# The written order of the attention steps, in a fused attention and mixture-of-experts kernel

## The chip, the cores and the metric

One NeuronCore of a Trainium2 chip runs the whole program. The metric is the device time of one execution in microseconds (us); less is better.

## The reference, cut to what matters

```python
q_s = exp(q - max(q, axis=-1)); q_s /= sum(q_s, axis=-1)        # softmax over the head dimension
k_s = exp(k - max(k, axis=2));  k_s /= sum(k_s, axis=2)         # softmax over the sequence
kv  = einsum('bhsd,bhse->bhde', k_s, v)
x   = einsum('bhsd,bhde->bhse', q_s, kv)                        # 8 batches, 8 heads, 576 tokens, 64 wide
x   = x.transpose(0, 2, 1, 3).reshape(4608, 512)
expert = argmax(x @ w_gate); gate = softmax(x @ w_gate)[expert] # 8 experts, top one
y[token] = gate * (relu(x @ w1[expert]) @ w2[expert])           # 512 -> 1024 -> 512
```

All inputs and the output are float32.

## The kernel before, in words

The program has two stages. The first is the attention with the routing, batch after batch (0 to 7). The second runs the experts over the routed rows, expert after expert, and is a stretch of matmuls that TensorE works through without a pause.

In the first stage nothing is scheduled at run time. The work is cut into 780 named steps, each on one engine, and the string `ORDER` lists the names in the order in which the instructions are written. Each name stands for the next step of its kind, by batch and then by part. An engine runs its own instructions strictly in the written order, and each waits for its inputs and for its buffers, so what stands behind a waiting instruction on that engine waits too. Between engines the order has no force of its own.

Below, KV.4.3 is part 3 of batch 4 of step KV. The steps, with their lines:

- SyncE issues the loads: LK (keys, L170; three buffers, so K of batch b waits for the KV steps of batch b-3), LV (values, L174; one buffer, so V of a batch waits for VP and VQ of the batch before), LQ (queries, L186; two buffers), CD (gate weights), CZ (zero rows), WG (eighths of the first expert's w1, L677), IL (the first expert's rows, L721), SW and VG (the first expert's w2, L689).
- Keys: KM0 and KM1 (VectorE, maxima over a partition's tokens, L316, L317, L320), KM2 (TensorE transposes, L325), KM3 (VectorE, L329), KM4 (TensorE spreads the maxima, L334), KS (VectorE subtracts, four parts, L350), KE (ScalarE exp, L354), KV (TensorE, L370, L375), N0 and N1 (VectorE, the denominator, L382, L385), N2 (ScalarE writes the scaled kv, L392), G0 to G3 (the product of kv with the gate weights: TensorE L399, ScalarE L403, TensorE L409, ScalarE L413).
- Values: VP, VQ (ScalarE copies, L178, L181).
- Queries: QM (VectorE, row maxima, L443), QS and QSR (GpSimd subtracts, L449, L455), QE (ScalarE exp of one slice, L460), TR and TL (TensorE transposes, L494), EX and EL (ScalarE, L489, L498).
- Output tiles: MM (TensorE, L509, L512, L515; it needs EX and G3), RE and EV (VectorE evicts, L519, L523, L527). MM has two output buffers: a tile waits for the EV of the tile two before it.
- Routing: LS, R0, R8, R1, R3, R4, R6, RB, RC, RD (VectorE, L577 to L620), R9 (ScalarE, L609), R5 (TensorE, L598 to L601), RH and PU (GpSimd, L624 to L632). PU scatters the rows of one tile to their expert's place in HBM; between two scatters GpSimd writes a dummy (L629).
- First expert: WH (ScalarE, L681) and WL (GpSimd subtracts, L686) split w1 into a high and a low part; IC and ID count its rows; IT, IH, IX bring its rows in; L1, L2, L3 (TensorE L740, ScalarE L745, VectorE L748) are its first layer's first five parts; VH, VL split w2.
- WM are 40 matmuls of constants at the start and WE five at the end (TensorE, L703, L708); nothing reads them.

The scatters of batch 7 come after the stage. At its end stands a barrier of all engines (L966), which also waits until the scatters have landed. Then TensorE goes on with the first expert: L740 again, L1111, and the transposes of L1028, for which the rows of the next step must have been read back from HBM.

Of the kernel before, what the change touches and what calls it, by code (L numbers as in the profile page):

```python
# [1592 lines left out]
```

## Time and profile before

| | us |
|---|---|
| three executions | 574.37, 574.82, 576.01 |
| median | 574.82 |
| the profiled execution, its own time | 575.68 |
| its span, first to last instruction | 573.9 |
| TensorE busy in the span | 544.8 (95%) |
| VectorE busy in the span | 314.1 (55%) |
| ScalarE busy in the span | 256.3 (45%) |
| GpSimd busy in the span | 147.7 (26%) |

The span leaves out 1.8 us of the execution's time, before the first and after the last instruction. Shares of busy time are means over two unlike stages. In the timeline rows, a bracket at the end is the idle time of the engine just before the instruction and what ended it; DVE is VectorE, ACT ScalarE, POOL GpSimd, PE TensorE, PEld its weight load, SPq the issue of a transfer by SyncE.

### The profile page before, as it was taken

To read this page: it belongs to the slowest core of one execution; us is meant where nothing else is said; L and a number is where in the kernel's file an instruction comes from. 1 tells how busy PE (TensorE), PEld (TensorE's weight loads), DVE (VectorE), ACT (ScalarE), POOL (GpSimd) and SP (SyncE) were. 2 spreads that over 40 slices of the span, in tenths; PEclk is the share of its full clock that TensorE was granted. 3 is DMA by queue.
4 is the path that set the end of the run, shared out by engine and by line. 5 is a ranking of instruction groups with operands and counts; after the bars stand their busy time and mean duration, and the time that the engine had idled before them with its cause. 6 is when DMAs were issued, how large, how long until landed. Compare 5 with 4: busy or idle time off the path is not lost.

```text
span 573.9 us, 12179 instructions
## 1 busy us (share of the span) xinstructions
PE 544.8 (95%) x3891; PEld 482.7 (84%) x3892; DVE 314.1 (55%) x644; ACT 256.3 (45%) x602; POOL 147.7 (26%) x237
## 2 busy tenths in 40 slices
PE   6799887998999999999999999999999999999995
PEld 2577776897978989899898989897999899898973
DVE  5899989797781431635223141436734473647250
ACT  0699987786412322534131323334725262534341
POOL 4224697685751010110201001002010201120021
PEclk9799999999999999999999999999999999999998
DMA  8989999753668932041931202031195229324700
GB/s 268 334 270 318 318 344 365 242 216 129 241 243 273 365 76 59 0 110 40 396 95 53 57 18 74 19 74 37 46 374 154 83 72 396 64 64 161 314 36 10
DMA packets 70272, 97.70 MB, mean 170 GB/s; under 512 B 9052, under 2 KB 50526, under 8 KB 69600
## 3 DMA queue, kind: packets, MB, share of 16 engines
q1 hardware_dynamic: 63760, 77.19, 42.2%
q0 software_dynamic: 5904, 19.03, 8.7%
q10 hardware_dynamic: 576, 1.07, 0.5%
q8 instruction: 19, 0.31, 0.2%
q14 instruction: 13, 0.11, 0.1%
HBM read 75.31 MB, written 22.34 MB: 170 GB/s over the span
## 4 chain that ended last, share of the span: by engine, by line
PE 75%; issue 0%; POOL 0%; ACT 0%; DVE 0%; POOLq 0%; SPq 0%
PE py L1059 31%; PE pt L1043 16%; PE ph L1043 16%; PE py L1111 3%; PE ph L740 3%; PE py L1099 1%; PE xp L512 1%; PE pt L1087 1%; PE qT L494 0%; PE pt L740 0%; PE pt L1072 0%; PE ph L1072 0%; PE pt L1028 0%; PE pt L726 0%; PE xp L515 0%
## 5 line engine op out<-in xcount | busy, mean ns | idle before, releaser
L1059 PE MATMUL py<-w2h,hid 128*128 128x512 f32 x528 | 164.9, 389 | 0.0
L1059 PEld LDWEIGHTS py<-w2h,hid 128*128 128x128 f32 x528 | 99.1, 188 | 20.4
L1414 POOL DMA_INDIRECT out<-yt,ix x36 | 40.7, 1131 | 284.6 <-ACT yt L1225 278.0
L1059 PE MATMUL py<-w2l,hid 128*128 128x512 f32 x264 | 102.9, 390 | 0.0
L1321 DVE SCALAR_TENSOR_TENSOR hid<-pt,hid 128x384 fp32r<-128x384 f32 x52 | 28.9, 556 | 125.1 <-ACT hid L1235 124.9
L1225 ACT ACTIVATE yt<-py,ga 128x512 f32<-128x512 f32 (+1 forms) x38 | 25.7, 678 | 134.0 <-PE py L1059 120.0
L1321 DVE SCALAR_TENSOR_TENSOR hid<-ph,hid 128x384 fp32r<-128x384 f32 x52 | 29.0, 558 | 53.3 <-ACT hid L1235 53.2
L1059 PEld LDWEIGHTS py<-w2l,hid 128*128 128x128 f32 x264 | 49.5, 188 | 9.8
L1310 DVE STREAM_TRANSPOSE xx<-xb 128x1536 f32<-128x1536 f32 x13 | 37.9, 2914 | 18.2 <-issue 18.2
L512 PE MATMUL xp<-kx,qTs 128*128 128x146 f32 x256 | 43.7, 312 | 2.1 <-ACT kx L413 2.0
L632 POOL DMA_INDIRECT xs<-xr,posi x36 | 37.0, 1029 | 22.0 <-issue 20.2
L512 PEld LDWEIGHTS xp<-kx,qTs 128*128 128x128 f32 x256 | 35.9, 194 | 5.8 <-ACT kx L413 2.4
L1043 PE MATMUL pt<-xh,w1h 128*128 128x384 f32 (+4 forms) x208 | 39.8, 313 | 0.2 <-issue 0.2
L1043 PE MATMUL ph<-xh,w1h 128*128 128x384 f32 (+4 forms) x208 | 39.6, 312 | 0.0
L1043 PE MATMUL pt<-xl,w1h 128*128 128x384 f32 (+4 forms) x208 | 39.6, 312 | 0.0
L1043 PE MATMUL ph<-xh,w1l 128*128 128x384 f32 (+4 forms) x208 | 39.6, 312 | 0.0
L1043 PE MATMUL pt<-xh,w1l 128*128 128x384 f32 (+4 forms) x208 | 39.6, 312 | 0.0
L1043 PE MATMUL ph<-xl,w1h 128*128 128x384 f32 (+4 forms) x208 | 39.5, 312 | 0.0
L1234 ACT ACTIVATE hf<-pt 128x64 f32<-128x64 f32 x52 | 11.7, 225 | 55.8 <-PE pt L1043 43.3
L1234 ACT ACTIVATE hf<-ph 128x64 f32<-128x64 f32 x52 | 11.7, 224 | 53.0 <-PE ph L1043 53.0
L1043 PEld LDWEIGHTS pt<-xh,w1h 128*128 128x128 f32 x208 | 33.6, 189 | 1.7 <-issue 0.7
L1043 PEld LDWEIGHTS pt<-xl,w1h 128*128 128x128 f32 x208 | 33.3, 189 | 0.0
(269 smaller groups left out, 988.8 us busy)
## 6 DMA issues: line engine op xcount, KB each, us to landing
raw<-in_moe_w SPq DMA_DIRECT2D x10, 2048.0 KB, 13.7
rawc<-in_moe_w SPq DMA_DIRECT2D x5, 2048.0 KB, 8.5
kt<-in_k SPq DMA_DIRECT2D x14, 640.0 KB, 8.3
xb<-xs SPq DMA_DIRECT2D x32, 192.0 KB
qt<-in_q SPq DMA_DIRECT2D x8, 640.0 KB, 8.8
vs<-in_v SPq DMA_DIRECT2D x8, 640.0 KB, 7.7
qt<-in_q SPq DMA_DIRECT2D x8, 512.0 KB, 7.3
vs<-in_v SPq DMA_DIRECT2D x8, 512.0 KB, 8.5
```

The source lines that it names most:

```text
L512: nc.tensor.matmul(xv[:, c, :KW], o.qT[i][:, c, :], kx[:, c, :], **flags)
L632: s = nc.gpsimd.indirect_dma_start(out=xs, out_offset=bass.IndirectOffsetOnAxis(ap=n.pi[:, t - t0:t - t0 + 1], axis=0), in_=xr[:, t, :], i ...
L740: m = nc.tensor.matmul(ph, wt[:, c, f * P:(f + 1) * P], xt[:, c, :], start=(n == 0), stop=(n == 3 * NC - 1))
L1043: m = e.matmul(ph, wt[:, c, f * P:(f + 1) * P], xt[:, c, :w], start=(n == 0), stop=(n == 3 * NC - 1))
L1059: m = e.matmul(g.PY[u], ht[:, f, u * P:(u + 1) * P], wt[:, f, :], start=(n == 0), stop=(n == 3 * NF - 1))
L1087: m = e.matmul(y[d * SLIM:(d + 1) * SLIM, :DM // 2], g.HT[:, i * P + s * SLIM:i * P + (s + 1) * SLIM], g.RAW2[:, 4 * s + i, d * DM // 2:(d ...
L1111: m = e.matmul(g.PY[u], ht[:, f, u * P:(u + 1) * P], wt[:, f, :], start=(n == 0), stop=(n == 3 * NF - 1))
L1225: m = e.activation(g.YT[u][:, :w], g.PY[u][:, :w], AF.Copy, scale=g.GA[:, u + thin:u + thin + 1]).wait_op(sPY[u], cu[u], GE)
L1234: e.activation(g.HF[:, f, :], g.PH[f][:, 2 * P:2 * P + SLIM], AF.Relu).wait_op(sPH[f], it, GE)
L1310: e.transpose(g.XX, g.XB.rearrange("p t (a c) -> p c t a", c=NC)).wait_op(sB, bs, GE)
L1321: e.scalar_tensor_tensor(g.HL[:, f, :], g.PH[f][:, :W], 0.0, g.HH[:, f, :].bitcast(F32), op0=ALU.max, op1=ALU.subtract).wait_op(sHH[f], it ...
L1414: e.indirect_dma_start(out=g.out, out_offset=bass.IndirectOffsetOnAxis(ap=g.IX[:, u:u + 1], axis=0), in_=g.YT[u], in_offset=None, bounds_c ...
```

## The change

Only the string `ORDER` differs. Every step is still there once; no step, tile, buffer or loop changes. What moves, engine by engine, where it is spoken of later:

| engine | before | after |
|---|---|---|
| PE, start | 15 WM, KM2.0, KM4.0, 22 WM, KM2.1, KM4.1, WM, TR.0.0, KV.0.0 to KV.0.3, TL.0 | 30 WM, KM2.0, 3 WM, KM4.0, 2 WM, KM2.1, KM4.1, TL.0, KV.0.0, KV.0.1, TR.0.0, 3 WM, KV.0.2, KV.0.3 |
| ACT, start | VQ.0, VP.0, QE.0.0, KE.0.0, ... , QE.0.2, EL.0, N2.0, EX.0.1, G1.0, G3.0, QE.0.3, VP.1 | KE.0.0 to KE.0.3, VP.0, VQ.0, EL.0, KE.1.0, QE.0.0 to QE.0.3, EX.0.0, ..., N2.0, EX.0.1, G1.0, G3.0, VP.1 |
| ACT, batches 4 to 6 | KE.5.2, VQ.6, G3.4, KE.5.3, VP.6 | KE.5.1, KE.5.2, G3.4, VQ.6, KE.5.3, KE.6.0, VP.6 |
| DVE, batch 5 | QM.5, KM3.6, ..., KS.6.3, ..., N0.5, R3.3, N1.5, R4.3, EV.4.0 | QM.5, EV.3.3, KM3.6, ..., KS.6.3, R8.3, RE.4.0, R1.3, EV.4.0, R3.3, R4.3, RC.3, N0.5 |
| DVE, batch 7 | R6.4, LS.5, R0.5, R8.5, R1.5, R3.5, R4.5, QM.7, N0.7, RE.6.0, N1.7, RB.5, EV.6.0 | LS.5, R0.5, R8.5, R1.5, QM.7, N0.7, N1.7, RE.6.0, EV.6.0, RE.6.1, R6.4, EV.6.1, ID, R3.5, T4, RE.6.2, EV.6.2, R4.5 |
| POOL, batch 2 | QS.1.0, QSR.1, QSR.2, QS.1.1, WL (1st), QS.2.0, QS.2.1 | QS.1.0, QSR.1, QS.1.1, QS.2.0, QSR.2, RH.0, WL (1st), QS.2.1 |
| POOL, batches 4 to 7 | PU.3.0, WL (6th), ..., PU.4.3, WL, WL, QS.7.0, QSR.7 | PU.3.0, ..., PU.4.3, WL, WL, WL, QSR.7, QS.7.0 |
| POOL, end | RH.5, QS.7.1, RH.6, PU.5.0 to PU.5.4, IN, PU.6.0, PU.6.1, RH.7, RH.7, PU.6.2, PU.6.3 | RH.5, QS.7.1, IN, RH.6, PU.5.0 to PU.5.4, RH.7, PU.6.0, RH.7, PU.6.1, PU.6.2, PU.6.3 |
| SyncE, end | LV.6, LK.7 (1st half), WG, LQ.6, LK.7 (2nd half), WG, LV.7, LQ.7, WG, IL | WG, LV.6, WG, WG, LQ.6, LK.7, LV.7, LQ.7, IL |

The diff:

```diff
@@ -33,25 +33,25 @@
 WARM_END = 5
 ON_ACT = (1, 1, 1, 1, 1, 1, 1, 1)
 ORDER = """
-WM WM WM WM WM WM WM WM WM WM WM WM LK WM WM LK LK LK KM0 KM0 LK LK WM LQ LQ LV LV KM1 KM2 KM3 CS KM4 KM0 VQ LK LK LQ KS KM0 KS
-CD WM WM WM WM WM WM WM WM WM WM WM LQ VP WM KM1 WM WM WM WM WM WM WM WM QM QS KS WM LV WM QE KE KE QE KE KS QSR KM2 KM3 KM4 KS
-KS KS WM TR KV KS KE KE EX QE KM0 KM0 KV KV KV N0 TL WM N1 KM1 KM2 KM3 EL TR QM N2 EX G0 KM4 KS QS QS LV KS KS G1 G2 WM G3 MM QE
-RE VP KS EV VQ LK KE LK KM0 KM0 LQ LQ KE KE KE KE TR MM RE KV WG LV EX QE QE QSR KV KV KV N0 N1 TR TR MM EX EV EX TR KM1 QE KM2
-QM N2 MM EX RE KM3 EV RE G0 QE EV LS R0 G1 QSR WH KM4 KS KS KS KS LV QS G2 WL VQ TL G3 MM RE LK VP KE EL KV MM KV KE LK KM0 TR
-WG LQ LV QS KV TR EV KE KE LQ R8 KM0 R1 KM1 LV KE KV N0 R3 EX EX WG KE LK N1 R9 KM2 RE EV KM3 QE N2 QE MM QS RE R4 EV TR QM KM4
-KS EX WH WL QSR KS KS R5 WG MM RE RB VQ KS EV MM RE R6 VP G0 LK G1 CZ KE KE QS WH WH QE KV KV EV LV LV KV TR TR EX TR G2 RC WL
-QE EX LS R0 KV LQ LQ KM0 R8 N0 G3 N1 TR KE N2 R1 RD R3 KM0 WG MM MM R4 RE KM1 R5 EX EV RE RB KM2 KM3 EV R6 MM VQ EX R9 RD RE EV
-LK VP LV G0 G1 QE MM WH RH TR TR WL PU EX QE PU PU PU RE RC QS EX QM KV KV TR EV QE QE KM4 KE KS WL LS QSR KS G2 KE QS R0 LV LK
-G3 KV KV EX N0 KS KS MM MM KE RE R8 TR QE VP EV VQ EX LQ LQ LV LV R1 N1 RE R3 EV RH PU PU PU TL EL QE MM LK WG KM0 TR MM R4 EX
-R5 RE KM0 EV PU R9 TR PU RC N2 EX RB MM G0 G1 RE TR QE EX RH R6 RD KM1 QS KM2 KV KV EV PU G2 QE QM KE VQ KM3 KM4 G3 MM QS PU KE
-VP RE WH EV KS KS KS TR LS LQ LQ KS R0 QSR EX LK WG PU PU KE LV KV KE MM KV RE R8 R1 N0 TR R3 N1 R4 RH R9 KE EX QE EV RC TR EX
-RE N2 LV R5 MM RB EV RD MM G0 QE QE QM KV TR G1 KV KE G2 QS RE EV KV EX PU WH KM0 G3 RE KM0 TR EV R6 KV QE LS N0 R0 N1 R8 KM1 R1
-EX MM MM TR N2 R9 RE R3 WL EX R4 R5 EV RB RE RD VP VQ PU EV KM2 KM3 MM RC RE PU TR EX LQ EV QSR KM4 KS KE MM KS RE PU KE PU G0
-G1 LQ KS KE RH QS EV MM RE KS EV QE R6 KV G2 KV PU QS PU G3 QE QE TR EX LS KV KE TR R0 PU PU WG EX WH R8 WL WL MM TL EL R1 KV R3
-R4 QM N0 RE N1 R5 TR QS QSR RB EV MM QE TR RE EX EV MM N2 G0 RE EV EX RD TR MM RE QE QE EX G1 IC ID TR QE G2 TR G3 EX EV LS R0
-MM R6 R8 R1 R3 R9 RH QS IL EX R4 QE RH IT IT RE RC PU PU PU PU R9 SW VG RC MM EV PU IH IH IX VG R6 RE TR EX IX MM EV R5 TR EX RE
-EV IT LS IH IX MM RE MM RB EV L1 R0 R8 R1 RE VH EV T4 R3 LS R0 R8 R1 R9 IN RD PU L2 IM L3 L1 R4 R3 VG R4 R6 L1 VL R6 VH L2 L2 R9
-L3 VG VH T0 L3 T1 PU L1 VL R5 RB RC RC L2 L3 L1 R5 RB RD RH RH RD L2 L3 PU PU WE WE WE WE WE
+WM WM WM WM WM WM WM WM WM WM WM WM WM WM WM WM WM WM WM WM WM WM WM WM WM WM WM WM WM WM LK LK KM0 LK LK KM0 KM1 LK LK KM2 KM3
+WM WM WM LQ CS KM4 KS KE KM0 KS KM0 KS KE KS KE KE KM1 LQ QM WM WM KM2 KM3 KM4 KS KS QSR KS KS LV LV TL LK VP CD LK LQ LQ VQ LV
+EL KE LV KV QS KM0 KV KM0 TR QS QE QE QE QE WM WM WM KV KV EX KM1 N0 N1 WM KM2 WM LK LK TR KE KE LQ KM3 N2 G0 QM EX G1 TR QS KM4
+KS KS KS QSR G2 G3 MM MM VP KS VQ KV RE QE EX QE EV KM0 RE KE QE QE LQ TR KV KV KM0 EX KE KE LV LV EV KV N0 TR TR WG EX KM1 N1
+N2 MM EX QM KM2 KM3 LK LK MM G0 G1 RE VQ KM4 EV G2 KS KS KS QS LQ LQ QS KS WG G3 MM RE RE QSR TL EV EV LS VP LV QE QE QE LV KE
+KE KV KV KV KM0 QE R0 KM0 R8 KE WH EL KM1 R1 KV N0 R3 N1 TR R4 EX MM RE EV KM2 TR MM RH N2 R5 EX WG KM3 WL LK TR EX G0 CZ VQ QS
+QM QS G1 RE VP EV KM4 MM RE MM LK KS KS WH R9 EV KE KE WG KS KS WH TR RE EV KV KV RB TR LS WL LV LV RC LQ LQ KE KE WL QE EX RD
+PU WG R0 R8 KV KV LK KM0 N0 PU N1 G2 EX G3 PU QE KM0 R1 N2 TR MM RE TR EX MM R9 QE R3 KM1 KM2 EX R6 R4 RH EV RE EV VQ MM R5 RC
+KM3 RB RE EV RD VP MM WH G0 G1 LV LV RE EV QM QS PU LK QSR KV TR WH WL WL EX G2 G3 TR TR LS EX EX QE KM4 KS KS KE MM RE KS KS EV
+KE KE KV KV MM R0 R8 R1 LQ MM LQ PU KE RE R3 QS QE EV R6 RE WG VQ VP LV LV R9 QSR TR KV TR EX PU QE PU MM QE PU QE KM0 R4 TL R5
+N0 WG WG EV RC EX TR N1 N2 MM KM0 EL RE RB EX TR EX G0 KM1 KM2 G1 R6 RD G2 KV QM EV RH PU WH KM3 KE KE QS LQ PU G3 KM4 VQ KE RE
+MM KV EV QSR TR MM KS KS QS LS QS KE VP KS PU KV R0 KS R8 RE R1 EV LQ TR R3 R4 QE KV EX R9 RC EX R5 KE N0 RE N1 N2 KE QE MM TR
+EX KE RB EV RD MM KV LK G0 LK G1 PU PU LV RH LV KV QM WH TR RE G2 TR KM0 EV R6 RE EV PU PU KM0 KV QE G3 QE MM EX EX KV LS KM1 R0
+RE MM R8 EV VP QSR VQ PU PU R1 R9 KM2 TR EX N0 PU R3 R4 RH N1 N2 RE KM3 EV MM RC R5 RB RE RD EV TR EX KM4 KS KS KS KE KE WH QS
+LQ PU KS PU MM G0 KE G1 MM RE EV RE EV LS R0 KE R8 R1 KV TR QS PU KV LQ QM G2 EX TL KV TR KV N0 PU QE G3 MM EL N1 EX QE TR RE EV
+MM RE QE QE R6 WL WL TR EX MM WL IL QSR N2 EV IC ID R3 TR T4 RE EX EX EV G0 G1 QS MM TR R4 RH RE EV LS QE R0 R8 R1 R9 G2 EX G3
+QE TR EX QE QS R5 RB R3 QE RC R4 IN SW VG VG VG RD RH PU MM IT IT RE EV IH IH IX MM RE TR EX IX MM EV R6 RE TR EX IT MM IH EV LS
+IX R9 RE R0 EV R8 R1 VH R9 R5 MM RE EV LS R3 R6 R4 RB RD L1 R0 RC R8 R1 L1 L2 L2 RC L3 R9 VH R3 VH IM L1 R4 L3 L2 PU PU PU PU R6
+R6 L3 RC T0 T1 VL VL L1 VG R5 RB L1 L2 L3 RD R5 RB RD L2 RH PU RH L3 PU PU PU WE WE WE WE WE
 """
 KD, ROW, LW, EO, LIVE, SMALL, WIDE, REST = range(8)
 NFLD = 5
```

## Rows read from the trace of the kernel before

**Rows 1.** The page's span in 40 equal slices: mean busy share, in tenths, of the 16 DMA engines.

```profile
DMA  8989999753668932041931202031195229324700
```

**Rows 2.** The chain that ended last, in order of time: start, us, what.

```profile
133.91 0.66 PE qT L494 x4
...
158.85 0.65 issue
...
177.45 1.71 PE pt L1028 x12
```

**Rows 3.** Timeline of TensorE, the first 30 us: start, us, instruction, count, idle before.

```profile
3.08 5.21 PE L703 MATMUL hot<-ones 128*128 128x512 bf16 x15 [3.08 <-DVE eps L231]
10.12 0.66 PE L325 MATMUL kmT<-ident,km 128*128 128x128 f32 x4 [1.83 <-DVE km L320]
...
12.05 4.91 PE L703 MATMUL hot<-ones 128*128 128x512 bf16 x22
...
21.73 1.12 PE L334 MATMUL mb<-ident,mx 128*128 128x128 f32 x4 [4.07 <-DVE mx L329]
...
24.27 3.90 PE L375 MATMUL kv<-vt,kt 128*64 128x65 f32 x80
```

**Rows 4.** Timeline of VectorE, 12 to 126 us.

```profile
12.60 0.69 DVE L316 TENSOR_TENSOR kp<-kt 128x512 f32<-128x512 f32 x1 [0.39 <-DMA kt<-in_k]
...
28.23 0.17 DVE L382 TENSOR_REDUCE own<-kv 128x4 f32<-128x8 f32 x1
...
29.99 0.69 DVE L329 TENSOR_REDUCE mx<-kmT 128x4 f32<-128x512 f32 x1 [0.81 <-PE kmT L325]
...
85.14 0.69 DVE L316 TENSOR_TENSOR kp<-kt 128x512 f32<-128x512 f32 x1 [1.52 <-DMA kt<-in_k]
...
103.74 0.17 DVE L382 TENSOR_REDUCE own<-kv 128x4 f32<-128x8 f32 x1 [3.80 <-PE kv L375]
...
106.06 2.81 DVE L443 TENSOR_REDUCE qm<-qt 128x40 f32<-128x2560 f32 x1
...
125.22 2.84 DVE L594 TENSOR_TENSOR oh<-dec,own 128x40 bf16<-128x40 f32 x1
```

**Rows 5.** Issue of transfers by SyncE, 28 to 36 us.

```profile
28.25 2.33 SPq L170 DMA_DIRECT2D kt<-in_k  x2
33.76 1.28 SPq L186 DMA_DIRECT2D qt<-in_q  x2
```

**Rows 6.** Timeline of ScalarE, 83 to 98 us.

```profile
83.31 2.01 ACT L178 ACTIVATE vt<-vs 128x1024 f32<-128x1024 f32 x2 [2.18 <-DMA vs<-in_v]
...
96.75 0.64 ACT L181 ACTIVATE vt<-vs 128x512 f32<-128x512 f32 x1 [3.39 <-DMA vs<-in_v]
```

**Rows 7.** Timeline of TensorE, 97 to 132 us.

```profile
97.55 0.77 PE L512 MATMUL xp<-kx,qTs 128*128 128x146 f32 x4 [1.96 <-ACT kx L413]
...
99.59 1.35 PE L375 MATMUL kv<-vt,kt 128*64 128x65 f32 x20
...
102.89 0.80 PE L375 MATMUL kv<-vt,kt 128*64 128x65 f32 x20
...
128.12 0.18 PE L598 MATMUL rk<-oh,before 128*128 128x40 bf16 x1 [0.44 <-DVE oh L594]
...
131.95 0.16 PE L509 MATMUL xp<-eps,ones 128*128 128x4 bf16 x1 [1.36 <-DVE xr L527]
```

**Rows 8.** Timeline of GpSimd, 125 to 156 us.

```profile
125.50 2.50 POOL L686 TENSOR_TENSOR w1l<-xt,w1h 128x512 fp32r<-128x512 f32 x2
...
139.96 1.01 POOL L632 DMA_INDIRECT xs<-xr,posi  x1 [4.79 <-issue]
...
155.32 1.04 POOL L632 DMA_INDIRECT xs<-xr,posi  x1 [0.19 <-issue]
```

**Rows 9.** Stretches: us, busy PE, PEld, DVE, ACT, POOL (counts), granted clock, DMA share, GB/s.

```profile
24.00:27.00 3.00, 3.00 (x52) 2.73 (x52) 2.93 (x6) 3.00 (x7) 0.00 (x0) 0.50 0.98 288
27.00:30.00 3.00, 2.65 (x47) 2.22 (x44) 2.04 (x6) 2.28 (x10) 0.00 (x0) 0.96 0.69 213
```

## The prediction

> **What bounds the kernel now.** I read the chain that ended last first, because it says where a change can reach the end. From 133.91 us on it is TensorE almost alone; at 158.85 it has 0.65 us of "issue", the barrier between the two stages, and from there it is matmuls again up to the last microseconds [rows 2]. Everything behind the barrier is untouched and keeps its length, so the question is only when the barrier is passed. The transposes that start at 177.45 need rows that a chain from the barrier brings back from HBM; both sides of that meeting start at the barrier and shift together.
>
> Then the timelines of the stage. VectorE's idle pieces between 24 and 84 us are 0.81 us at most, then come 1.52 and 3.80 us [rows 4]. The DMA engines are nearly full through the first hundred microseconds (slices of 14.3 us: 8, 9, 8, 9, 9, 9, 9 tenths) [rows 1], with a hollow at 0.69 after 27 us [rows 9]. So up to about 106 us VectorE paces the stage, fed by the loads, and from there TensorE has work nearly without a break. The reader is to see three kinds of lost time: VectorE waiting for a load or for TensorE, VectorE stretched by GpSimd, and TensorE kept dry by both.
>
> Comparing the two written orders by engine, I found a good place to compare: when VectorE begins QM.6 (106.06 before [rows 4]) it has done the same 154 steps in both orders. What differs up to there is only how long it stood or was stretched. TensorE at MM.4.3, close by, has also done the same set in both. All terms are worked out against the profiled execution, 575.68 us, which is 0.86 above the median of 574.82; the forecast for the median is the same difference taken from 574.82.
>
> **The change part by part.**
>
> *The start.* Thirty dummies now stand ahead of KM2.0, not fifteen. The first fifteen take 5.21 us from 3.08; later ones take 4.91/22 = 0.223 each [rows 3]. So KM2.0 begins at 3.08 + 5.21 + 15 x 0.223 = 11.6, not 10.12. Before, VectorE waited 0.39 us for K of batch 1 [rows 4], which absorbs that much: **+1.1 us**. It could be 0 if the dummies were quicker, and more by what the first rival says. In exchange KE.0 runs before the values land, which ends ScalarE's idle start, but KV.0.2 and KV.0.3 now stand behind KM4.1, TL.0, TR.0.0 and three dummies. KM4.1 comes 1.1 us after its 21.73, so by about 22.8; TL.0 waits for QM.0 and QSR; four KV parts took 3.90 us and started at 24.27 [rows 3]. With TL.0 done near 24.5, two KV parts at 1.35, TR.0.0 at 0.66, the dummies at 3 x 0.223 and two parts at 0.80 [rows 3, 7], KV.0.3 ends near 30.1 instead of 28.2 (an estimate). N0.0 (28.23 before [rows 4]) then makes VectorE wait about 0.4 us, and KM3.2 after it 0.4 more instead of 0.81: 0 in sum.
>
> *The loads.* K of batch 3 waits for KV.0.3, so it is issued near 30.1 rather than 28.25, later. But Q of batch 2, which was issued only at 33.76 [rows 5] since it waited for QE.0.3, now follows directly, because QE.0.0 to QE.0.3 stand together ahead of N2.0. The hollow of rows 9 thus gets longer at its front and is closed at its back. From there the same bytes stand ahead of V of batch 5 in both orders. QS.1.1 no longer stands behind QSR.2, so Q of batch 3 can leave sooner too. I take loads of batches 5 and 6 to land 2 to 3 us sooner. That removes VectorE's 1.52 us wait at 85.14 for K of batch 6 [rows 4]: **-1.5 us**, between 0 (nothing lands sooner) and -1.52.
>
> *G3.4 ahead of VQ.6.* Before, ScalarE waited 3.39 us for V of batch 6 [rows 6]; G3.4 stood behind that, MM.4.0 behind G3.4 (1.96 us idle [rows 7]), KV.5.2 and KV.5.3 behind MM.4.0, and N0.5 behind them: the 3.80 us at 103.74 [rows 4]. Now G3.4 goes first, and N0.5 stands behind EV.4.0, R3.3, R4.3 and RC.3, which used to follow it. What is late next is MM.4.0 by KM4.6, which VectorE itself feeds through QM.5 and KM3.6. I leave 0.5 us of the wait: **-3.3 us**, between 0 and -3.8.
>
> *GpSimd's subtractions move.* One stall is plain in the rows: R4.5, which reads two SBUF tiles, took 2.84 us, and it ended with two WL steps on GpSimd that began at 125.50 and took 1.25 us each [rows 4, 8]. In the new order the first WL moves behind QS.2.0, QSR.2 and WH, to about where KM0.4, R8.0, KM1.4 and R1.0 run on VectorE. I add one WL: **+1.25 us**, between 0 and 2.5 (QS.2.1 follows it at once).
>
> The Trainium skill's page SBUF — State Buffer, "Who interferes with whom", says that a VectorE instruction with two SBUF inputs and a GpSimd instruction that reads SBUF exclude each other for the whole instruction, whoever starts first. The trace agrees: R4.5's 2.84 us against 2.50 us of WL. By that rule the sum would take the first WL and QS.2.1 behind it in full; by the row, what VectorE meets of them.
>
> *K of batch 7* now stands behind Q of batch 6 and two more WG. Its first half was issued before Q of batch 6. KM0.7 stands right behind QM.6 and RE.4.2, so VectorE may meet a load not yet there. I add **+0.7 us**, between 0 and 1.5 (the size of the wait at 85.14).
>
> Sum at KM0.7: 1.1 - 1.5 - 3.3 + 1.25 + 0.7 = -1.75.
>
> *QM.7 ahead of R4.5.* Before, R4.5's stall and the 2.81 us of a QM [rows 4] stood ahead of EV.6.0, and TensorE waited 0.44 us for R4.5 and 1.36 us for EV.6.0 [rows 7]. Now QM.7, N0.7, RE.6.0 and EV.6.0 go first; R4.5 follows EV.6.2, and R5.5 stands just ahead of MM.7.0. Cover for it: routing of batch 5 is needed only by PU.5.0. **-1.8 us**, between 0 and -1.8.
>
> *The end of the stage.* PU.5.0 began at 139.96, after RC.5 [rows 8]. Now RD.5 comes about as late, after R4.6. Nine scatters follow in either order, the last beginning at 155.32; the barrier was passed after 158.85. TensorE's and VectorE's last steps keep their order, and the first expert's rows keep about the slack they had. **0**, between -0.65 (the whole issue time) and +1 (one scatter's busy time).
>
> Total: -1.75 - 1.8 = **-3.55 us**: 575.68 - 3.5 = 572.2 for a profiled execution like this one, 571.3 for the median.
>
> **The rivals.**
>
> *The start costs in full (slower).* TensorE stood still 4.07 us before 21.73 [rows 3], and the granted clock was 0.50 at 24 to 27 us [rows 9]; that is 1.2 of 2.4 GHz. The new order leaves it idle longer there, since KM2.1 waits for KS.0 and KM0.1 behind a late start. If the clock stays low through KV.0.3, two KV parts cost 1.35 instead of 0.80 each [rows 7], so +1.1, and three dummies double to +0.65. KV.0.3 ends 1.8 + 1.1 + 0.65 = 3.55 us later, K of batch 3 leaves and lands later by as much, and the full DMA engines pass that on: the waits of 1.52 and 3.80 come back. Sum 3.55 + 1.25 - 1.8 = +3.0, 577.8. It decides if K of batch 3 lands after about 39 and nothing later catches up. Against it: Q of batch 2 closes the hollow.
>
> *Three WL in a row stop R8.5 (no change).* Three WL now follow PU.4.3, 3.75 us in one piece where two were 2.50 [rows 8]. R8.5 and R1.5 read two SBUF tiles each and stand shortly ahead of R4.5, where WL began. If PU.4.3 is done a little sooner against VectorE, R8.5 waits 3.75 us and QM.7 behind it. Then instead of -1.8 there is + (3.75 - 2.65), and 574.82 - 1.75 + 1.1 = 574.2. The Trainium skill's page named above, same section, is the rule behind this rival: the second to start is blocked until the first ends.
>
> *The last scatters set the barrier (no change).* If PU.5.0 does not move forward from 139.96, because RD.5 now waits for R4.6, RB.5 and R5.5, the scatters end and land as before, TensorE's lead ends in a wait at the barrier, and the time stays 574.8. For it: the scatters follow each other closely. Against it: RD.5 hangs on VectorE's own progress, which is what gets faster.
>
> *More is gained.* No new stall and no late K: 1.1 - 1.52 - 3.8 - 1.8 - 0.65 = -6.7, 568.1.
>
> **How the numbers follow.** Chances: the forecast 0.48, more 0.08, WL in a row 0.20, the scatters 0.08, the start 0.16. The time is 571.3; its own range, each term at half its spread, is 569.5 to 573.0. For 8 in 10 I go from 568.8, leaving out half of "more", to 577.0, leaving out about half of the slow case. Three per mille, 1.7 us, is about what a measurement can tell from no change: faster 0.56, same 0.28, slower 0.16.
>
> **What the next profile would show.** Right: the first L740 matmul after the barrier near 156 instead of 159.50; QM.6 beginning near 104; VectorE's idle before N0.5 gone and G3.4 ahead of the copy of V of batch 6; no VectorE step near 125 us stretched to 2.84 us; KM2.0 near 11.6. Wrong: KV.0.3 ending after 31 with the clock still at 0.50; a wait for a load at KM0.7 above 1.5 us; a stretched R8.5; or TensorE idle for more than 1 us before the barrier while scatters are still landing.

## The result, and the profile after

| | before | after |
|---|---|---|
| executions on one chip | 574.26 to 576.01 (6) | 577.27 to 579.64 (6) |
| median, us | 574.69 | 578.84 |
| the profiled execution, its own time | 575.68 | 577.61 |
| its span | 573.9 | 575.8 |
| TensorE's mean granted clock | 0.988 | 0.982 |

The new order is slower: 1.0065 of before, 95% interval 1.0041 to 1.0089, or 2.4 to 5.1 us. The forecast was 571.3, with a range from 568.8 to 577.0.

One number of each trace gives nearly the whole time: the first L740 behind the barrier, at 159.50 before and here at

```profile
161.74 0.97 PE L740 MATMUL pt<-xh,w1h 128*128 128x384 f32 x4 [0.74 <-PE hote L708]
```

From there to the end of the execution it is 416.2 us before and 415.9 after, and 415.9 to 416.3 in the traces of all runs below but e6 (417.9). Two marks split the way to it: where VectorE begins QM.1 (batch 1) and QM.6. Before, QM.6 began at 106.06 [rows 4]. Timeline of VectorE of the new kernel (columns as in [rows 3]):

```profile
53.68 1.25 DVE L585 TENSOR_TENSOR pe<-own,lm 128x32 f32<-128x32 f32 x1
54.86 1.59 DVE L320 TENSOR_TENSOR km<-km,kt 128x512 f32<-128x512 f32 x1
...
73.14 0.17 DVE L382 TENSOR_REDUCE own<-kv 128x4 f32<-128x8 f32 x1 [2.26 <-PE kv L375]
...
81.57 2.81 DVE L443 TENSOR_REDUCE qm<-qt 128x40 f32<-128x2560 f32 x1
...
106.84 0.17 DVE L382 TENSOR_REDUCE own<-kv 128x4 f32<-128x8 f32 x1 [0.38 <-PE kv L375]
...
108.05 2.81 DVE L443 TENSOR_REDUCE qm<-qt 128x40 f32<-128x2560 f32 x1
...
117.21 2.25 DVE L585 TENSOR_TENSOR pe<-own,lm 128x32 f32<-128x32 f32 x1
...
129.14 0.22 DVE L585 TENSOR_TENSOR pe<-own,lm 128x40 f32<-128x40 f32 x1
...
129.51 2.81 DVE L443 TENSOR_REDUCE qm<-qt 128x40 f32<-128x2560 f32 x1
...
135.76 2.13 DVE L786 SCALAR_TENSOR_TENSOR base<-m,r,rb 8x1 f32<-8x1 f32 x1
```

The 3.80 us wait before N0.5 [rows 4] has become 0.38, as forecast. But QM.4 begins at 81.57, where it began at 74.34 before: 7.2 us are lost by there, and QM.6 is 2.0 late in spite of what is regained. In good part that is time which this trace of before lost itself, in its waits of 1.52 and 3.80 us. The loss begins with R8.0 and KM1.4 at 53.68. GpSimd at that time, and later:

```profile
53.37 1.51 POOL L686 TENSOR_TENSOR w1l<-xt,w1h 128x512 fp32r<-128x512 f32 x1 [5.85 <-ACT w1h L681]
54.85 1.04 POOL L449 TENSOR_TENSOR qs<-qt,qm 128x512 f32<-128x512 f32 x1
...
130.12 3.72 POOL L686 TENSOR_TENSOR w1l<-xt,w1h 128x512 fp32r<-128x512 f32 x3
133.81 1.05 POOL L455 TENSOR_TENSOR qsr<-qt,qm 128x512 f32<-128x512 f32 x1
134.83 1.91 POOL L449 TENSOR_TENSOR qs<-qt,qm 128x1024 f32<-128x1024 f32 x1
```

R8.0, 0.18 us long before, ends when the first WL ends; KM1.4, 0.69 long before, runs when QS.2.1 ends: 1.07 + 0.90 = 1.97 us. T4 (L786, at 135.76) is held in the same way till QS.7.1 has ended. The chain that ended last passes through both and shows what hangs on them:

```profile
53.76 1.17 DVE pe L585
54.93 1.51 DVE km L320
56.59 0.63 PE kmT L325 x4
...
58.01 1.18 PE xp L512 x4
59.20 1.18 PE xp L512 x4
...
66.11 1.46 DVE kt L350 x2
67.58 0.13 DVE qden L519
67.72 1.08 PE qT L494 x4
68.81 0.22 PE kv L370
69.03 2.16 PE kv L375 x40
```

TensorE stood 2.27 us before KM2.4 (56.59) and 2.78 us before TR.2.0 (67.72), which needs the buffer that KS.4.3 frees. In this order KV.3.0 stands behind TR.2.0; before, TR.2.0 stood behind KV.3.2. After each stop the granted clock is at the lower level, 1.2 GHz, and an L512 group takes 1.18 instead of 0.61. Stretches of the new kernel (columns as in [rows 9]):

```profile
53.00:56.00 3.00, 1.32 (x11) 1.07 (x9) 2.97 (x4) 1.04 (x3) 2.53 (x2) 1.00 1.06 357
57.00:60.00 3.00, 3.00 (x17) 2.85 (x15) 2.97 (x5) 2.37 (x9) 0.00 (x0) 0.53 1.06 389
...
67.00:70.00 3.00, 2.28 (x25) 1.89 (x27) 2.93 (x11) 2.50 (x6) 1.30 (x2) 0.57 0.98 342
```

From 10 us to the barrier the clock was at the lower level at 20.4 to 27.2 and 98.9 to 102.3 before, and at 16.2 to 26.4, 57.2 to 60.6 and 67.4 to 70.8 in the new kernel.

### The profile page after: what moved, and what is told of

The parts are those of the page before. It is cut to its first block, busy times and chain, and to the rows that moved or that the text cites. A ratio compares the mean times of both kernels' runs of the same rounds, so it can differ in the third digit from the quotient of the medians.

```text
span 575.8 us, 12174 instructions
## 1 busy us (share of the span) xinstructions
PE 546.4 (95%) x3891; PEld 484.3 (84%) x3892; DVE 318.8 (55%) x644; ACT 257.0 (45%) x602; POOL 147.9 (26%) x238
## 3 DMA queue, kind: packets, MB, share of 16 engines
q10 hardware_dynamic: 576, 1.07, 0.5%
## 4 chain that ended last, share of the span: by engine, by line
PE 84%; DVE 10%; issue 2%; ACT 1%; DMA 1%; SPq 0%; POOL 0%; POOLq 0%; ACTq 0%
PE py L1059 31%; PE pt L1043 16%; PE ph L1043 16%; PE xp L512 4%; PE py L1111 3%; PE ph L740 3%; PE kv L375 2%; PE qT L494 2%; DVE kt L350 2%; PE hot L703 2%; DVE xr L527 1%; DMA qt<-in_q 1%; PE py L1099 1%; DVE qm L443 1%; DVE kp L316 1%
## 5 line engine op out<-in xcount | busy, mean ns | idle before, releaser
L1059 PEld LDWEIGHTS py<-w2h,hid 128*128 128x128 f32 x528 | 99.1, 188 | 20.4
L1321 DVE SCALAR_TENSOR_TENSOR hid<-ph,hid 128x384 fp32r<-128x384 f32 x52 | 29.0, 558 | 53.3 <-ACT hid L1235 53.2
L512 PE MATMUL xp<-kx,qTs 128*128 128x146 f32 x256 | 44.3, 314 | 0.2 <-ACT kx L413 0.2
L512 PEld LDWEIGHTS xp<-kx,qTs 128*128 128x128 f32 x256 | 36.3, 196 | 1.6 <-ACT kx L413 0.3
```

What stands on the lines that cost most here:

```text
L512: nc.tensor.matmul(xv[:, c, :KW], o.qT[i][:, c, :], kx[:, c, :], **flags)
L1059: m = e.matmul(g.PY[u], ht[:, f, u * P:(u + 1) * P], wt[:, f, :], start=(n == 0), stop=(n == 3 * NF - 1))
L1321: e.scalar_tensor_tensor(g.HL[:, f, :], g.PH[f][:, :W], 0.0, g.HH[:, f, :].bitcast(F32), op0=ALU.max, op1=ALU.subtract).wait_op(sHH[f], it ...
```

## The experiments

Theories: **Lock**, the hold of R8.0 and KM1.4 beside the first WL and QS.2.1 starts the loss; **Start**, the thirty dummies and the low clock behind them lose it; **Late**, what stands behind QM.6 loses it. Two came with the first results: **Slot**, TR.2.0 ahead of KV.3.0; and **Clock**, the half clock behind TensorE's stops.

The marks of every trace are together here, in us, with the ratio of all timed executions to those of before on the same chip (95% interval). Executions of before had medians of 571.9 to 574.2 on those chips and ranged from 570.3 to 579.9, so one trace can stand some us off its kernel's median.

| kernel | QM.1 | QM.6 | QM.1 to QM.6 | QM.6 to barrier | ratio |
|---|---|---|---|---|---|
| before | 30.60 | 106.06 | 75.46 | 53.44 | 1 |
| after | 30.72 | 108.05 | 77.33 | 53.69 | 1.0065 (1.0041, 1.0089) |
| e1_wl_back | 31.32 | 112.05 | 80.73 | 53.66 | 1.0112 (1.0058, 1.0166) |
| e2_start | 31.95 | 104.16 | 72.21 | 52.17 | 0.9989 (0.9959, 1.0018) |
| e3_late | 30.40 | 103.02 | 72.62 | 53.70 | 1.0007 (0.9975, 1.0039) |
| e4_wl_moved | 31.03 | 106.87 | 75.84 | 52.24 | 0.9986 (0.9958, 1.0014) |
| e5_kv3_first | 31.98 | 106.93 | 74.95 | 58.94 | 1.0068 (1.0044, 1.0092) |
| e6_dummies | 32.44 | 107.65 | 75.21 | 59.63 | 1.0133 (1.0085, 1.0180) |
| e7_g34 | 29.99 | 106.11 | 76.12 | 52.19 | 0.9985 (0.9964, 1.0005) |
| e8_late_fix | 29.87 | 103.12 | 73.25 | 52.76 | 1.0006 (0.9986, 1.0025) |
| e9_mid_only | 31.90 | 107.52 | 75.62 | 52.17 | 1.0114 (1.0076, 1.0151) |
| e10_kv3_qm7 | 31.14 | 107.29 | 76.15 | 60.79 | 1.0198 (1.0176, 1.0219) |
| e11_all_fixes | 31.70 | 102.70 | 71.00 | 63.10 | 1.0189 (1.0166, 1.0211) |
| e12_best | 30.62 | 105.14 | 74.52 | 52.11 | 1.0025 (1.0003, 1.0047) |
| e13_mid_fixed | 31.33 | 101.28 | 69.95 | 56.78 | 0.9985 (0.9959, 1.0012) |
| e14_mid_wl | 32.35 | 106.64 | 74.29 | 52.42 | 1.0008 (0.9984, 1.0031) |
| e15_routing5 | 31.83 | 109.21 | 77.38 | 53.33 | 1.0064 (1.0043, 1.0086) |
| e16_all_new | 32.81 | 104.73 | 71.92 | 52.99 | 0.9994 (0.9969, 1.0019) |
| e17_r84 | 32.60 | 105.59 | 72.99 | 56.83 | 1.0059 (1.0025, 1.0094) |
| e18_r84_k7 | 31.42 | 104.08 | 72.66 | 56.86 | 1.0086 (1.0061, 1.0110) |

**Four parts, each by itself.** The diffs of the experiments are the written orders of the engines.

```diff
 e1, in the new order
-ACT  VQ.2 G3.1 VP.2 ... KE.3.0 WH.0 EL.2
+ACT  WH.0 VQ.2 G3.1 VP.2 ... KE.3.0 EL.2
-POOL QS.1.1 QS.2.0 QSR.2 RH.0 WL.0 QS.2.1
+POOL QS.1.1 WL.0 QS.2.0 QSR.2 QS.2.1 RH.0
 e2, in the order of before: the start of the new one
 e3, in the order of before: the new one from QM.6
 e4, in the order of before
-POOL WL.0 QS.2.0 QS.2.1       ACT  G1.1 WH.0 VQ.2 ... KE.3.2 EX.1.2
+POOL QS.2.0 WL.0 QS.2.1       ACT  G1.1 VQ.2 ... KE.3.2 WH.0 EX.1.2
```

> The new order with one thing put back: WH.0 stands again behind G1.1, the first WL ahead of QS.2.0, and QS.2.1 right behind QSR.2, so GpSimd is done with them before R8.0 and KM1.4. Theory Lock (the loss begins where the first WL and QS.2.1 hold R8.0 and KM1.4, 2.0 us, and grows by what is late behind them up to 75 us): about 575.3 us, between 573.5 and 576.8; R8.0 near 0.2 us, KM1.4 near 0.7, TensorE's 2.27 us ahead of KM2.4 gone. Theory Start (the 30 dummies and the clock at half lose it): unchanged, 578.8 within 0.8. Theory Late (the order behind QM.6 loses it): unchanged, 578.8.

> The order of before, with only the start of the new one: VectorE up to KM3.2, TensorE up to KV.1.3, ScalarE up to VQ.1, GpSimd up to QSR.1, SyncE up to Q of batch 2. Theory Lock: about 575.0 us, within 0.8 of before, since QM.1 begins at most 0.4 us later. Theory Start: 577 to 578.5. Theory Late: as before, 574.7.

> The order of before up to QM.6 on VectorE, MM.4.2 on TensorE, QE.5.1 on ScalarE, QS.5.1 on GpSimd and the last WG on SyncE; from there the new order (QM.7 ahead of R4.5, three WL in a row, IN and RH moved). By the prediction's own terms for this part: 573.0 us (-1.8). Theory Lock: between 573.0 and 575.2, the latter if R8.4 and T4 are held by GpSimd here too (2.25 and 2.13 us in the new kernel). Theory Late: 577 or more.

> The order of before with one thing of the new one: WH.0 moved behind KE.3.2 and the first WL moved behind QS.2.0, with QS.2.1 behind it, so that they run while VectorE is at KM0.4 and KM1.4. Theory Lock: 576.7 us or a little more (+2.0 of VectorE held, part of it absorbed or passed on); L317 and L320 of batch 4 stretched beyond 1 us. Theories Start and Late: as before, 574.7, within 0.8.

e1 went the wrong way. The hold of R8.0 and KM1.4 was gone, as was the stop before KM2.4, but the WL had moved into the way of QSR.2, and TensorE now stopped for that. Timelines of TensorE and GpSimd in e1:

```profile
51.18 0.98 PE L494 MATMUL qT<-ident,qsr 128*128 128x128 f32 x4 [1.88 <-POOL qsr L455]
```

```profile
46.95 1.28 POOL L686 TENSOR_TENSOR w1l<-xt,w1h 128x512 fp32r<-128x512 f32 x1 [8.79 <-ACT w1h L681]
48.19 1.92 POOL L449 TENSOR_TENSOR qs<-qt,qm 128x1024 f32<-128x1024 f32 x1
50.07 1.05 POOL L455 TENSOR_TENSOR qsr<-qt,qm 128x512 f32<-128x512 f32 x1
```

The clock was at half from 51.4 to 54.8, and again behind the stop before TR.2.0, which was still there (2.51 us) although the hold was gone. So e1 traded one stop for another and settles nothing on the lock. e2 says that the start costs nothing: theory Start falls. e3 says that the new late order brings nothing: 53.70 us, where 51.6 was expected. In e4 the WL began at 53.45, during KM1.4, which kept its 0.69 us; the WL took 1.69 instead. The meeting had not taken place, so e4 is no test either.

**The second stop, the clock, G3.4, the late part.**

```diff
 e5, in the new order
-PE   MM.1.4 TR.2.0 KV.3.0 KV.3.1 TR.2.1
+PE   MM.1.4 KV.3.0 KV.3.1 TR.2.0 TR.2.1
 e6, in the new order
+PE   9 dummy matmuls ahead of KM2.4, 18 short ones ahead of TR.2.0
 e7, in the order of before
-ACT  VQ.6 G3.4                 DVE  N0.5 R3.3 N1.5 R4.3 EV.4.0 RC.3 RE.4.1
+ACT  G3.4 VQ.6                 DVE  EV.4.0 R3.3 R4.3 RC.3 N0.5 RE.4.1 N1.5
 e8, as e3, and
-DVE  R8.4 EV.5.0 R1.4 N0.6 R3.4 R4.4 N1.6 RE.5.1 KM3.7 EV.5.1
+DVE  EV.5.0 N0.6 N1.6 RE.5.1 KM3.7 EV.5.1 R8.4 R1.4 R3.4 R4.4
-DVE  T4 RE.6.2 EV.6.2 R4.5     PE   R5.4 TR.5.4 KM4.7
+DVE  RE.6.2 EV.6.2 R4.5 T4     PE   TR.5.4 KM4.7 R5.4
```

> The new order with one step moved on TensorE: KV.3.0 and KV.3.1 stand ahead of TR.2.0, as they did before. Theory Slot (TR.2.0 waits for the buffer that KM4.4 fills and that only KS.4.3 frees, 2.78 us in the new kernel, and KV.3 and N0.3 now stand behind it): KV.3.0 begins near 65 instead of 68.6, N0.3 near 70 instead of 73.1, the time falls by 2 to 3 us to about 576.3. Theory Clock (what costs is that TensorE's clock falls to half behind each of its stops): the same if the stop gets short, else unchanged. Theory Lock (R8.0 and KM1.4 held by GpSimd): unchanged, 578.8 within 0.8.

> The new order unchanged, with dummy matmuls of constants added in TensorE's two stops: 9 of 512 columns ahead of KM2.4 and 18 of 264 ahead of TR.2.0, about 2.0 us in each, into tiles that the next steps overwrite. No step can begin earlier by them; they only keep TensorE busy. Theory Clock: no half clock between 54 and 71, and the time falls by 1.5 to 3.5 us to about 576. Theories Lock and Slot: the waits are there as before, 578.8 within 0.8, or slightly more.

> The order of before with one part of the change alone: G3.4 ahead of VQ.6 on ScalarE, and N0.5, N1.5 behind EV.4.0, R3.3, R4.3 and RC.3 on VectorE. By the prediction's term (-3.3): about 570.5 on a chip where before takes 573.4, the wait before N0.5 0.5 us or less. Rival: the wait goes elsewhere (V of batch 6, KV.6, MM.4.0 by KM4.6) and less than 1 us is gained.

> The order of before up to QM.6 and the new one from there, as in the earlier run with the late part alone, which gained nothing, with two things changed: R8.4, R1.4, R3.4 and R4.4 stand behind EV.5.1 (R5.4 behind KM4.7), away from QS.6.0, and T4 stands behind R4.5, away from QSR.7 and QS.7.0. Theory Lock late (R8.4 held 2.25 us by QS.6.0 makes TensorE wait about 1.5 us for EV.5.0 and eats the gain of QM.7 ahead of R4.5): from QM.6 to the barrier 52 us instead of 53.7, about 572.3. Rival: the moved steps meet another subtraction, or the stage's end is set elsewhere: 574 as in that run.

e6 was to show what the clock does. The same two stretches as above:

```profile
57.00:60.00 3.00, 3.00 (x23) 2.47 (x22) 2.97 (x10) 1.27 (x6) 1.28 (x1) 1.00 0.89 270
...
67.00:70.00 3.00, 2.59 (x51) 2.03 (x49) 2.93 (x12) 2.41 (x6) 1.30 (x2) 1.00 1.00 351
```

The clock stayed at 2.4 GHz, and from QM.1 to QM.4 it took 47.52 us instead of 50.85 (before: 43.74); at QM.6 2.1 us of that were left. But this does not show that the dummies did it. In this execution KM1.4 kept its 0.68 us, and QS.2.1 held R1.0 behind it instead, so KM2.4 could begin sooner. e9 (below), with the same steps up to there and no dummies, met GpSimd in the same way. Timelines of VectorE, GpSimd and TensorE in e9:

```profile
56.14 0.68 DVE L320 TENSOR_TENSOR km<-km,kt 128x512 f32<-128x512 f32 x1
56.74 1.04 DVE L588 SCALAR_TENSOR_TENSOR ge<-pe,dec 128x32 f32<-128x32 f32 x1
```

```profile
56.13 1.60 POOL L449 TENSOR_TENSOR qs<-qt,qm 128x512 f32<-128x512 f32 x1
```

```profile
56.97 0.63 PE L325 MATMUL kmT<-ident,km 128*128 128x128 f32 x4 [1.37 <-DVE km L320]
```

There too the clock stayed up, and QM.1 to QM.4 took 47.50. Which of the two steps is held hangs on little: KM1.4 and QS.2.1 begin 0.01 us apart both here (56.14, 56.13) and in the new kernel (54.86, 54.85). So theory Clock is left open, and in time e6 is no faster than the new order (1.0133 of before).

e5 took 45.83 to QM.4, with R1.0 held as in e6, and had 2.4 us left at QM.6. The traces of both lost it, and more, behind QM.6: first R8.4, held 2.26 us in e5, stopped TensorE for 1.82 us, and the clock was at half from 120.5 to 123.9; then came the rival of the prediction in which the three WL hold R8.5. Timelines of VectorE and GpSimd in e5:

```profile
128.37 4.43 DVE L585 TENSOR_TENSOR pe<-own,lm 128x40 f32<-128x40 f32 x1
```

```profile
128.01 0.97 POOL L632 DMA_INDIRECT xs<-xr,posi  x1 [0.18 <-issue]
129.00 3.73 POOL L686 TENSOR_TENSOR w1l<-xt,w1h 128x512 fp32r<-128x512 f32 x3
```

TensorE then waited 2.28 us, and the clock fell to half at 137.6. This trace is of an execution of 581.9 us. Ten of the twelve of e5 took 575.0 to 577.8, two 581.9 and 582.5; what keeps the ten some 4 us above before, no trace shows.

e7 is the forecast's largest term alone. The wait before N0.5 was gone, but other waits of VectorE stood in its place, and QM.6 began at 106.11, as before (106.06):

```profile
86.67 0.69 DVE L316 TENSOR_TENSOR kp<-kt 128x512 f32<-128x512 f32 x1 [2.21 <-DMA kt<-in_k]
91.60 0.19 DVE L613 TENSOR_TENSOR rs<-rk,oh 128x32 f32<-128x32 f32 x1 [1.52 <-PE rk L601]
```

Twelve executions give -0.9 us (-2.1 to +0.3) where -3.3 was forecast. e8 took the holds of R8.4 and T4 out of the late part: 52.76 us instead of 53.70, and no change in the time that the interval could tell.

**The early half alone, and the three WL.**

```diff
 e9: the new order up to QM.6, the order of before from there
 e10, as e5, and
-DVE  R8.5 R1.5 QM.7 N0.7
+DVE  QM.7 R8.5 R1.5 N0.7
 e11, as e10, with R8.4 and T4 as in e8, and
-ACT  KE.3.0 WH.0 EL.2 EX.1.2 N2.2 EX.1.3       POOL WL.0 QS.2.1
+ACT  KE.3.0 EL.2 EX.1.2 N2.2 EX.1.3 WH.0       POOL QS.2.1 WL.0
 e12, as e2, with G3.4 and N0.5 as in e7, and
-DVE  R4.5 QM.7 N0.7 RE.6.0 N1.7 RB.5 EV.6.0 RE.6.1 EV.6.1
+DVE  QM.7 N0.7 RE.6.0 N1.7 EV.6.0 R4.5 RE.6.1 EV.6.1 RB.5
```

> The new order up to QM.6 on VectorE, MM.4.2 on TensorE, QE.5.1 on ScalarE, QS.5.1 on GpSimd and the last WG on SyncE; from there the order of before. Theory Middle (the new order loses 2 to 5 us between QM.3 and QM.4, and gives only part of it back by QM.6): 1.5 to 3.5 us above before. Theory Late (what the new order loses, it loses behind QM.6, where three WL in a row hold R8.5): as before, within 0.8; from QM.6 to the barrier 52.2 us instead of 53.7 to 59.

> The new order with two moves: KV.3.0 and KV.3.1 ahead of TR.2.0 as in the earlier run, and QM.7 ahead of R8.5, so that the three WL run while VectorE reduces one operand. Theory Late: R8.5 is no longer stretched to 4.4 us, no execution lies above 580 (where the run without the second move had two of twelve above 581), median 575 to 576. Rival: the three WL hold the next two-input step (R8.5 or R1.5 behind QM.7) as long, QM.7 was not the point, and the high executions stay.

> The new order with every meeting that the traces showed taken out: KV.3.0 and KV.3.1 ahead of TR.2.0; the first WL behind QS.2.1 and its WH behind EX.1.3; R8.4, R1.4, R3.4, R4.4 behind EV.5.1 with R5.4 behind KM4.7; QM.7 ahead of R8.5; T4 behind R4.5. If those causes are all there is: within 1 us of before or under it (G3.4 ahead of VQ.6 is still in it). If something else in the new order costs: 575 or more.

> The order of before with the parts of the change that did no harm or should pay: the new start up to KM3.2; G3.4 ahead of VQ.6 with N0.5 behind RC.3; and QM.7 ahead of R4.5 alone (R4.5 behind EV.6.0, RB.5 behind EV.6.1, R5.5 behind MM.6.1), with no third WL. By the prediction's terms -3.3 and -1.8 would come: 5 us under before. By what the runs so far showed (each part alone within 0.2% of before): 0 to 2 us under before.

e9: the early half alone makes the kernel slower (theory Middle). Its six executions fall in two groups, 574.65 to 576.39 and 579.37 to 581.16, and the trace is of one of the shorter; the longer ones have no trace. e10 was meant to cure R8.5 and made it worse, in every execution (582.3 to 584.0): QM.7 done early lets GpSimd go from the WL straight on to QSR.7 and QS.7, and R8.5, which came while the WL ran, was held until the whole row had ended. Timelines of VectorE and GpSimd in e10:

```profile
131.01 6.20 DVE L585 TENSOR_TENSOR pe<-own,lm 128x40 f32<-128x40 f32 x1
```

```profile
129.38 3.74 POOL L686 TENSOR_TENSOR w1l<-xt,w1h 128x512 fp32r<-128x512 f32 x3
133.08 1.05 POOL L455 TENSOR_TENSOR qsr<-qt,qm 128x512 f32<-128x512 f32 x1
134.09 1.91 POOL L449 TENSOR_TENSOR qs<-qt,qm 128x1024 f32<-128x1024 f32 x1
135.95 0.18 POOL L624 COPY xr<-tok 128x5 f32<-128x5 f32 x1
136.10 1.05 POOL L449 TENSOR_TENSOR qs<-qt,qm 128x512 f32<-128x512 f32 x1
```

e11 has the same hold (6.17). e12, the parts that should pay put together, pays nothing; by its interval it is even a little slower than before.

**Telling the causes apart.** e13 is e9 with KV.3.0 and KV.3.1 ahead of TR.2.0 (as e5) and the first WL late (as e11); e14 is e9 with the WL alone. e15 is the new order with R8.5, R1.5, R3.5 and T4 behind EV.6.2; e16 the new order with the edits of e13, of e15 and R8.4 as in e8.

> The new order up to QM.6 with KV.3.0 and KV.3.1 ahead of TR.2.0, the first WL behind QS.2.1 and its WH behind EX.1.3; from QM.6 on the order of before. Theory Middle (these two are what the early half loses): 5 us or more under the earlier run with the new order up to QM.6 (577.9), so about 571 to 573, 1 us under before or equal to it; from QM.1 to QM.6 about 71 us, as in the run with all edits. Rival (something else early costs, such as later loads): 575 or more.

> As the run beside it, but with the first WL and its WH moved alone; TR.2.0 stays ahead of KV.3.0. Theory Lock (the hold of R8.0 and KM1.4 starts the loss): nearly all of the gain, 572 to 574. Theory Slot (TR.2.0 waits for the buffer until KS.4.3 has run, and KV.3 behind it): a small part of the gain, 575.5 to 577.

> The new order with R8.5, R1.5, R3.5 and T4 moved behind EV.6.2, ahead of R4.5, so that no step of VectorE with two SBUF inputs stands beside the three WL, QSR.7 and QS.7.0. Theory Row (R8.5 held there is what makes the new late order slow and its time jump): no execution above 580, from QM.6 to the barrier 52 to 53 us, the median 1 to 4 us under the new order measured on the same chip scale (1.0065 of before), so 1.000 to 1.004 of before plus what the early half costs. Rival: it is as slow as the new order, 1.006 or more, and the late loss lies in R8.4 beside QS.6.0 or elsewhere.

> The new order with the early edits (KV.3 ahead of TR.2.0, the first WL late), R8.4, R1.4, R3.4, R4.4 behind EV.5.1, and R8.5, R1.5, R3.5, T4 behind EV.6.2. If Middle and Row are all that costs: 570 to 573, at or under before. If something else in the new order costs: 575 or more.

The WL alone (with its WH, and QS.2.1 ahead of it) takes the early half from 1.0114 to 1.0008, 6 us (3.5 to 8.7 by the two intervals); KV.3 takes it to 0.9985, which the intervals don't tell from 1.0008. The first is beyond the intervals, though e9 rests on six executions. e15 is as slow as the new order: in that order, at its own pace, the row of WL costs nothing, and theory Row falls. e16, with all of it, is where before is (0.9994). From e15 to e16 that is 4.0 us (2.1 to 5.9), for the WL, KV.3 and R8.4 together; KV.3 alone gave nothing there (e5), and the WL alone was not run in the whole new order.

The traces tell the early causes apart better than the times do:

| up to QM.4 | traces | QM.1 to QM.4, us |
|---|---|---|
| the order of before (e2, e12: but for the start) | before, e2, e3, e4, e7, e8, e12 | 43.4 to 45.2 |
| the new order, KM1.4 held | after, e15 | 50.9 |
| the new order, R1.0 held instead | e6, e9 | 47.5 |
| KV.3 ahead of TR.2.0, KM1.4 held | e10 | 47.5 |
| KV.3 ahead of TR.2.0, R1.0 held instead | e5 | 45.8 |
| the WL late, TR.2.0 ahead of KV.3 | e14 | 47.8 |
| both moved | e11, e13, e16, e17, e18 | 44.1 to 44.3 |

So there are two causes of about the same size, some 3 to 4 us each where KM1.4 is held, and the second does not follow from the first: in e14, where the hold and the stop before KM2.4 are gone, TensorE still stops before TR.2.0. Timeline of TensorE in e14:

```profile
66.23 0.93 PE L494 MATMUL qT<-ident,qs 128*128 128x128 f32 x4 [2.76 <-DVE qden L519]
```

At QM.6 the two weigh otherwise: the way from QM.1 is 75.62 in e9, 74.29 in e14 and 69.95 in e13.

e13 had the earliest QM.6 of all, 101.28, and lost the lead behind it; the clock was at half from 115.4 to 118.8. Timelines of VectorE and TensorE in e13:

```profile
106.61 0.69 DVE L316 TENSOR_TENSOR kp<-kt 128x512 f32<-128x512 f32 x1 [1.55 <-DMA kt<-in_k]
...
111.58 1.90 DVE L585 TENSOR_TENSOR pe<-own,lm 128x32 f32<-128x32 f32 x1
```

```profile
114.69 0.19 PE L598 MATMUL rk<-oh,before 128*128 128x32 bf16 x1 [2.17 <-DVE oh L594]
```

The last two runs went for that:

```diff
 e17, as e13, and
-DVE  N1.6 R8.4 KM1.7 R1.4 RE.5.0 R3.4 R4.4 EV.5.0 RB.4 RE.5.1 RD.4 EV.5.1
+DVE  N1.6 KM1.7 RE.5.0 EV.5.0 RE.5.1 EV.5.1 R8.4 R1.4 R3.4 R4.4
-PE   R5.4 KM2.7                RB.4 and RD.4 behind EV.5.2
+PE   KM2.7 MM.5.2 TR.5.4 KM4.7 R5.4
 e18, as e17, and
-SP   LV.6 WG WG LQ.6 LK.7
+SP   LV.6 LK.7 (1st) LQ.6 LK.7 (2nd) WG WG
```

> The kernel with the new order up to QM.6 mended (KV.3 ahead of TR.2.0, the first WL late) and the order of before behind it, with the routing of batch 4 moved: R8.4, R1.4, R3.4, R4.4 behind EV.5.1, RB.4 and RD.4 behind EV.5.2, R5.4 behind KM4.7. If R8.4 beside QS.6.0 is what lost the lead: from QM.6 to the barrier 53 to 54.5 us instead of 56.8, about 571.5 us (0.4% under before). Rival (the load of K of batch 7 and the end of the stage set it): as without the edit, 0.9985 of before.

> The same, and K of batch 7 issued right behind V of batch 6, its second half behind Q of batch 6, both ahead of the last two WG. If the wait of 1.55 us for K of batch 7 set the rest: 1 to 1.5 us less than the run beside it, about 570.3. Rival: Q of batch 6 lands later and QM.6 with it, no gain.

R8.4, moved later, was held again by QS.6.0, for 2.58 us (e18: 2.57), since GpSimd came to it at that time too; TensorE stopped for 2.67 us in that time. Both runs came out slower than before (1.0059 and 1.0086). No kernel here is shown to be faster than before.

## Why the prediction was wrong

**The step that failed is "GpSimd's subtractions move", +1.25 us between 0 and 2.5.** The place was right, R8.0 and KM1.4; the hold was 1.97 us, within the bounds. Against before it is even less, 1.4: there KM0.4 (49.86) took 1.27 us beside QS.2, and 0.68 in the new kernel. The price left out what a hold of that length does further on: TensorE stops 2.27 us for KM2.4, its clock falls to half, and QM.4 is some 3 us late by this alone. By e9 and e14 this place is worth about 6 us of time in the early half (1.0114 against 1.0008); in the whole new order it can be no more than the 4 us between e15 and e16, unless the other two edits in e16 cost. How it comes to 6 in the time, where L740 begins only 0.6 apart in the traces of e9 and e14, stays open: the longer executions of e9 have no trace. Nor is the share of the half clock shown. The Trainium skill's rule that the prediction weighed (SBUF — State Buffer, "Who interferes with whom") would have put the WL and QS.2.1 in full there, 1.51 + 1.04 by the trace; against the 6 us of e9 and e14 that too would have been some 3.5 short. The prediction took R4.5 as agreeing with that rule; but R4.5 began at 125.22, 0.28 us ahead of the WL that it waited for, and by the rule the first to start is not held.

**TR.2.0 ahead of KV.3.0 had no term at all.** The table above gives it 3.7 us at QM.4 (e14 against e13), and 4.3 at QM.6. In the time it did not show: e13 lost it again behind QM.6.

**The parts do not add up.** The early half alone is 6.5 us above before (e9), the late half alone 0.4 (e3, -1.4 to +2.2), and both together 3.7.

**"G3.4 ahead of VQ.6", -3.3 us, was a wait and not time to be had.** The wait went, in the new kernel and in e7, and the time did not (-0.9, interval -2.1 to +0.3). In the profiled execution of before the clock was at half from 98.9 to 102.3, just ahead of N0.5, with KV.5.2 at 1.35 instead of 0.80 [rows 7]. In e3, which has the order of before up to there and no such stretch, the same wait was 2.52, and QM.6 began at 103.02. In e2, e4 and e8, with G3.4 as before too, it was 2.24 to 3.07: the wait is in every trace, its size in this one alone. In e7 VectorE waited elsewhere instead.

**"QM.7 ahead of R4.5", -1.8 us, likewise.** The 2.84 us of R4.5 [rows 4] were that execution's: the late order of before took 53.44 us there and 52.17 to 52.42 in e2, e4, e7, e9 and e14, where R4.5 took 1.60 to 1.63. e12, which has QM.7 ahead of R4.5 without the rest of the late part, took 52.11. The new late order took 53.3 to 53.7 in after, e1, e3 and e15: both of TensorE's waits [rows 7] were gone, and R8.4, held 2.25 us, had put one of 1.35 in their place. So the late part was +0.25 in the pair of traces and about +1.4 against the others.

**The start, +1.1.** The size was about right: QM.1 begins at 31.7 on the mean of the 15 traces with the new start and at 30.4 in the five with the old. In the pair of traces it was 0.12 only, and KM2.0 began at 10.97, not 11.6. It doesn't reach the end (e2: -0.6 us, -2.4 to +1.0). The first rival, that the start costs in full, was the slower case of the forecast; its sign came true by luck, since its mechanism did not: the clock was back at 26.4, and KV.0.3 ended near 29.2.

**The loads, -1.5.** VectorE's wait for K of batch 6 is gone, but not because the load comes sooner: its first half was issued at 73.17, where it was 68.80. VectorE itself came 5 us later.

**K of batch 7, +0.7:** no wait in the new kernel; where VectorE came sooner (e13), 1.55. **The end of the stage, 0:** right, 0.74 us of idle time at the barrier in both.

**Three WL in a row** did not stop R8.5 in the new kernel's trace, where it was through 0.8 us before the WL began, and did in the traces of e5 and e6, whose late order is the same: 4.43 and 4.41 us, where 3.75 had been forecast.

## What to carry to other kernels

Price a hold of one engine by what stands behind it: behind two microseconds on VectorE, TensorE stopped and its clock fell to half, and the next mark was some 3 us late, the time of the early half 6. Before a wait of a trace goes into a sum as time to gain, look how long it is in other executions, whether the clock was low ahead of it, and what the engine would wait for next. A meeting that hangs on hundredths of a microsecond needs more than one trace: with the same steps before it, QS.2.1 held KM1.4 in some executions and R1.0 in others. An order tuned to a fraction of a microsecond moves all its meetings when one part moves: of the seventeen written orders tried here none came out measurably ahead of before.
